# Which weight tiles of the last MLP are converted during attention, and which inside the MLP

## The chip, the cores and the metric

The kernel runs on one core of one Trainium2 chip. The metric is the device time of one execution in microseconds. A core has five engines that run their own instruction queues: TensorE (PE, matmul, with its weight loads shown apart as PEld), VectorE (DVE), ScalarE (ACT), GpSimd (POOL) and SyncE (SP, which here only issues DMAs). Each queue is worked off in the order in which it was written.

## The reference

Attention with a local window and 32 global tokens, a gated MLP with a convolution along the sequence, and a Fourier mixing stage with a second MLP. What this case touches is the last stage:

```python
def _moe2_ref(x, w_ch1, w_ch2):              # x: 4 x 576 x 512
    X = np.fft.fft(np.fft.fft(x, axis=1), axis=2)
    u = x + np.real(X)
    mu = np.mean(u, axis=-1, keepdims=True)
    var = np.mean((u - mu) ** 2, axis=-1, keepdims=True)
    un = (u - mu) / np.sqrt(var + 1e-06)
    ch = np.maximum(un @ w_ch1, 0.0) @ w_ch2  # 512 x 2048, 2048 x 512
    return u + ch
```

All weights arrive as 64-bit floats, and the kernel itself turns them into float32.

## The kernel before, in words

**Weight tiles.** The weights of the last MLP are 32 tiles, numbered 0 to 31: 0 to 15 are blocks of `w_ch1`, 16 to 31 of `w_ch2`. A tile arrives as 128 x 512 64-bit numbers (512 KB) and becomes two float32r halves, a rounded part and the remainder (512 KB as well), so that three matmuls give a product of nearly float32 accuracy. I call that a conversion. It is `unpack` (through `from_f64`) and `put`: on ACT L164, L167 and L200, on POOL L165, on DVE L171, L172 and L201. So it takes three instructions each of ACT and DVE, one of POOL.

**Where tiles are converted.** Twelve tiles are converted during attention, one in every second step (`keep_load`, `keep_make`, `keep_store`), and parked in DRAM as `kept`. Later `fetch_c` brings a kept tile back by a DMA that POOL issues (L724, `w_v<-kept`), finished, while a tile that was not kept comes in raw by a DMA that SP issues (L179), and `make_c` converts it.

**The boundary.** After attention, the end of the first MLP (`m_g1`, `m_conv`, `m_gate`, `m_g2`), the Fourier transforms of the four batches (`fft`, b = 0 to 3) and the first steps of the last MLP (`c_g1(v)`, then `c_g2(v - 2)`) are interleaved. A transform uses two banks of PSUM, `ps_s` and `ps_t`, in turn: a group of matmuls fills one, ACT and DVE (L665 and L666, L672 and L673) or DVE alone (L686, L689, L696, L699) empty it. The steps v = 0 to 4 (`NCONV`) of the last MLP carry the transforms of batches 1 to 3 and the conversions of tiles 8 to 19:

```python
order = [x for v in range(4) for x in (16 + v, 8 + v)] + [12, 13, 14, 15]
...
            for x in order[len(order) * v // NCONV:len(order) * (v + 1) // NCONV]:
                make_c(x)
```

From then on the last MLP is matmuls alone: 128 steps, eight chunks of 272 tokens by 16 hidden blocks. `c_g1(v)` multiplies by tile m = v mod 16 into the bank `ps_pv` or `ps_g`, ACT (L791) and DVE (L792) turn that into `hdt`, and `c_g2(v)` multiplies `hdt` by tile 16 + m. `ln` prepares the next chunk beside it (L745 to L773).

**Buffers.** Tiles 20 to 31 live in `fp`, in the slots of the transform's own constants and work tiles: 20 to 24 in those of `c2`, `s2`, `fh`, `fl` and `ff`, 25 and 26 in that of `c1`, 27 and 28 in that of `s1`, 29 to 31 in that of `ab`. They can be loaded only when the last transform has done with them. Tiles 16 to 19 live in `lw`, which takes over the space of the first MLP's work tiles. While the last MLP runs, the conversion's temporary is one of three places in `misc`.

**What sets the order.** SP and PE run in the order of the code up to the end of attention. Behind that a scheduler orders every engine's queue, by priorities (conversions of the last MLP, `cv`, 200; `fft` 100; `cev` 400) and its own idea of durations, so a change of the code can move instructions far from it.

Of the kernel before, what the change touches and what calls it, by code (L numbers as in the profile page):

```python
# [11 lines left out]
F32R = mybir.dt.float32r  # L12
BF16 = mybir.dt.bfloat16
I32 = mybir.dt.int32
# [16 lines left out]
SOLO = 8  # L31
LAG_G2 = 3
NCONV = 5
KEEP0, KEEP1 = 10, 20
NPB, NHB = 3, 3
MT = [(0, 92), (92, 92), (184, 90)]

# [88 lines left out]
def fused_kernel(ctx: ExitStack, tc: tile.TileContext, d, out):  # L126
    nc = tc.nc
    pe, act, dve, gp, sp = nc.tensor, nc.scalar, nc.vector, nc.gpsimd, nc.sync

    def pri(c):  # L130
        k = PRIORITY.get(c, 0)
        return tc.high_priority(offset=k) if k else nullcontext()

    def prio(c):
        def deco(f):
            def g(*a, **k):
                with pri(c):
                    return f(*a, **k)
            return g
        return deco  # L140
# [15 lines left out]
    def f32(ap):  # L156
        return ap.bitcast(F32)

    def bits(ap):
        return ap.bitcast(I32)  # L160
# [28 lines left out]
    def unpack(pool, t, *how):  # L189
        if mags:  # L190
            mag = mags.pop(0)
            mags.append(mag)
        else:
            mag = pool.tile([128, 512], F32, tag="mag", name="mag", bufs=2)
        from_f64(t.rearrange("p (c b) -> p c b", b=2), mag, *how)
        return mag
# [7 lines left out]
    def rows_of(w, m):  # L204
        return bits(w)[128 * m:128 * m + 128, :]
# [4 lines left out]
    def c_src(i):  # L210
        return cols_of(d["ch1"], i) if i < 16 else rows_of(d["ch2"], i - 16)
# [15 lines left out]
    mp = left.enter_context(tc.tile_pool(name="mp", bufs=2))  # L227
# [14 lines left out]

    def keep_tile(i, lag):
        k, odd = divmod(i - KEEP0 - lag, 2)
        return None if odd or not 0 <= k < 32 - KEEP1 else KEEP1 + k

    @prio("keep")
    def keep_load(x):
# [194 lines left out]
    w_raw, w_in, w_out = {}, {}, {}  # L443
# [181 lines left out]
    fp = right.enter_context(tc.tile_pool(name="fp", bufs=1, side="right"))  # L625
# [85 lines left out]
    ch1, ch2 = {}, {}  # L711

    def c_slot(i):
        return (wp, f"w{i}") if i < 16 else (lw if i < 20 else fp, f"v{i}")

    @prio("cv")
    def fetch_c(i, n=1):
        pool, tag = c_slot(i)
        if i not in kept:
            w_raw[i] = fetch(pool, tag, c_src(i))  # L720
            return
        t = pool.tile([128, n, 2, 512], F32R, tag=tag, name="w_" + tag)
        for j in range(n):
            gp.dma_start(t[:, j], kept[i + j])  # L724
            ch2[i + j - 16] = t[:, j]

    @prio("cv")
    def make_c(i):
        if i not in kept:
            t = put(*c_slot(i), unpack(mp, w_raw.pop(i), gp, True))  # L730
            (ch2 if i > 15 else ch1)[i % 16] = t

    ln_t, dead = {}, {}

    def ln(c):
# [96 lines left out]
    for u in range(ulast + 1, NM + LAG_G2):  # L832
# [15 lines left out]
        k = u - (NM - 8)  # L848
# [21 lines left out]
    for v in range(128 + 2):  # L870
        c, m = divmod(v, 16)
        if v < NCONV:
            while done * NCONV < nstep * (v + 1):
                step(f3)
                done += 1
                if nstep - done == 6:
                    for i in range(20, 25):
                        fetch_c(i)
            for x in order[len(order) * v // NCONV:len(order) * (v + 1) // NCONV]:
                make_c(x)  # L880
            if v == NCONV - 1:
                for i, n in ((25, 2), (27, 2), (29, 3)):
                    fetch_c(i, n)
                dead[1] = frp.tile([128, 4, 546], F32, tag="u", name="u")
        if m == (NCONV if c == 0 else 4) and c + 1 < 8:
            lnq.append(ln(c + 1))
        step(lnq)
        c_g1(v)
        c_g2(v - 2)
# [43 lines left out]
```

## Time and profile before

| | |
|---|---|
| time, median of 3 runs | 844.3 us (840.43 to 846.37) |
| time of the profiled execution | 842.18 us |
| its span, first to last instruction | 840.4 us |
| PE busy | 788.0 us (94%) |
| DVE busy | 460.1 us (55%) |
| ACT busy | 373.8 us (44%) |
| POOL busy | 197.9 us (24%) |
| mean granted clock of TensorE | 0.968 |

The shares are averages over stages that are limited by different things. Attention with the first MLP takes about 340 us, the boundary reaches from there to 471 us, and the rest is the last MLP. PE's clock is given as a share of 2.4 GHz; 0.50 is the lower of its two levels, 1.2 GHz.

### The profile page before, as it was taken

The numbers are of one execution on the slowest core, as the hardware profiler recorded it, in microseconds if no ns is written. First come the engines' busy times: TensorE is split into PE (matmuls) and PEld (weight loads), VectorE is DVE, ScalarE is ACT, GpSimd is POOL, SyncE is SP. The second block draws the span as 40 slices with busy tenths as digits, with TensorE's granted clock in tenths as the row PEclk, the third lists the DMA queues.
The fourth block names the chain that finished last, engine by engine and source line by source line (L and its number), as shares of the span: only waits on it lengthen the run. The fifth ranks groups of instructions, "written<-read, shape, count | busy, mean of one in ns | idle before, by whom it ended". The sixth has DMA issues, their size and how long they took to land.

```text
span 840.4 us, 16106 instructions
## 1 busy us (share of the span) xinstructions
PE 788.0 (94%) x6436; PEld 739.7 (88%) x6436; DVE 460.1 (55%) x1202; ACT 373.8 (44%) x949; POOL 197.9 (24%) x274
## 2 busy tenths in 40 slices
PE   5667999999999999999888999999999999999997
PEld 3445888888898889998777999999999999999997
DVE  5877986777777776688989531222222122222212
ACT  5666777676676675467764132121211212121110
POOL 3535332222222221001123252040402204030100
PEclk9787999999999999999969999999999999999999
DMA  9452034132322303025422700000000000000000
GB/s 315 162 190 78 34 127 143 50 142 83 110 99 93 101 26 103 8 87 164 142 110 55 247 27 1 2 27 1 28 1 28 1 2 27 1 28 1 27 2 28
DMA packets 28843, 60.93 MB, mean 72 GB/s; under 512 B 2344, under 2 KB 19112, under 8 KB 28768
## 3 DMA queue, kind: packets, MB, share of 16 engines
q1 hardware_dynamic: 26208, 50.95, 17.8%
q0 software_dynamic: 2560, 8.94, 3.5%
q8 instruction: 51, 0.84, 0.4%
q14 instruction: 24, 0.20, 0.1%
HBM read 49.52 MB, written 10.75 MB: 72 GB/s over the span
## 4 chain that ended last, share of the span: by engine, by line
PE 55%; DVE 19%; DMA 12%; ACT 10%; issue 2%; SPq 1%; POOL 0%; DVEq 0%; ACTq 0%
PE ps_a L143 25%; PE ps_g L143 14%; PE ps_pv L143 12%; DMA raw_r<-in_ch_dram 6%; PE ps_s L143 3%; DMA raw_w<-in_w_in_dram 3%; ACT pb L314 2%; DVE mag L171 2%; PE ps_t L143 2%; DVE y L487 2%; DVE pb L302 2%; DVE mag L172 2%; DVE w_w L201 1%; DVE y L488 1%; DVE g L507 1%
## 5 line engine op out<-in xcount | busy, mean ns | idle before, releaser
L143 PE MATMUL ps_a<-hdt,w_v 128*128 128x272 f32 x1536 | 214.6, 288 | 0.3 <-DVE w_v L201 0.3
L143 PEld LDWEIGHTS ps_a<-hdt,w_v 128*128 128x128 f32 x1536 | 201.5, 189 | 0.6 <-DVE w_v L201 0.6
L143 PE MATMUL ps_g<-xh,w_w 128*128 128x274 f32 x512 | 115.2, 304 | 3.3 <-ACT h L476 3.3
L325 POOL TENSOR_SCALAR pb<-pb,sm 128x224 f32<-128x224 f32 x128 | 76.5, 614 | 155.6 <-DVE sm L320 125.0
L143 PE MATMUL ps_a<-g,w_w 128*128 128x272 f32 x768 | 111.6, 292 | 0.1
L143 PE MATMUL ps_pv<-chl,w_w 128*128 128x272 f32 x768 | 108.0, 289 | 0.0
L143 PE MATMUL ps_g<-chl,w_w 128*128 128x272 f32 x768 | 107.8, 288 | 0.0
L143 PEld LDWEIGHTS ps_a<-g,w_w 128*128 128x128 f32 x768 | 101.5, 190 | 1.1 <-issue 0.5
L143 PEld LDWEIGHTS ps_pv<-chl,w_w 128*128 128x128 f32 x768 | 101.4, 190 | 0.0
L143 PEld LDWEIGHTS ps_g<-chl,w_w 128*128 128x128 f32 x768 | 100.7, 188 | 0.0
L143 PEld LDWEIGHTS ps_g<-xh,w_w 128*128 128x128 f32 x512 | 86.8, 193 | 11.7 <-issue 6.2
L792 DVE SCALAR_TENSOR_TENSOR hdt<-ps_pv,hdt 128x272 fp32r<-128x272 f32 x64 | 28.1, 440 | 123.2 <-ACT hdt L791 123.2
L792 DVE SCALAR_TENSOR_TENSOR hdt<-ps_g,hdt 128x272 fp32r<-128x272 f32 x64 | 28.0, 438 | 113.0 <-ACT hdt L791 113.0
L791 ACT ACTIVATE hdt<-ps_g 128x272 fp32r<-128x272 f32 x64 | 25.4, 397 | 137.3 <-PE ps_g L143 132.7
L791 ACT ACTIVATE hdt<-ps_pv 128x272 fp32r<-128x272 f32 x64 | 25.3, 396 | 137.4 <-PE ps_pv L143 133.1
L143 PE MATMUL ps_g<-xl,w_w 128*128 128x274 f32 x256 | 75.2, 294 | 0.0
L813 POOL TENSOR_TENSOR misc<-misc,u 128x272 f32<-128x272 f32 x28 | 19.3, 721 | 213.0 <-DVE misc L812 213.0
L314 ACT ACTIVATE pb<-pb,sm 128x224 f32<-128x224 f32 x128 | 60.3, 473 | 19.9 <-DVE sm L302 19.7
L143 PE MATMUL ps_s<-qk 64*128 64x224 f32 (+1 forms) x144 | 39.1, 427 | 13.2 <-DVE smg L396 6.1
L165 POOL TENSOR_SCALAR mag<-mag 128x512 f32<-128x512 f32 x36 | 24.5, 682 | 110.5 <-ACT mag L164 109.7
L143 PEld LDWEIGHTS ps_g<-xl,w_w 128*128 128x128 f32 x256 | 49.3, 193 | 0.0
L487 DVE SCALAR_TENSOR_TENSOR y<-h,convw,y 128x272 f32<-128x272 f32 x64 | 33.8, 529 | 25.0 <-ACT y L486 24.7
(207 smaller groups left out, 1269.9 us busy)
## 6 DMA issues: line engine op xcount, KB each, us to landing
qk<-in_qk_dram SPq DMA_DIRECT2D x16, 592.0 KB, 5.8
raw_w<-in_ch_dram SPq DMA_DIRECT2D x16, 512.0 KB, 3.7
raw_r<-in_ch_dram SPq DMA_DIRECT2D x12, 512.0 KB, 4.8
kept<-w_o SPq DMA_DIRECT2D x12, 512.0 KB, 3.0
w_v<-kept POOLq DMA_DIRECT2D x12, 512.0 KB, 4.8
v<-in_v_dram SPq DMA_DIRECT2D x8, 640.0 KB, 4.4
out_dram<-misc SPq DMA_DIRECT2D x32, 136.0 KB, 1.7
raw_w<-in_w_in_dram SPq DMA_DIRECT2D x8, 512.0 KB, 6.5
```

The source lines that it names most:

```text
L143: return pe.matmul(o, a, b, start=start, stop=stop)
L165: (clamp or dve).tensor_scalar(mag, mag, TOP, 2.0, op0=ALU.min, op1=ALU.max)
L171: dve.scalar_tensor_tensor(val, val, 3, tail, op0=ALU.logical_shift_left, op1=ALU.bitwise_or)
L172: dve.scalar_tensor_tensor(val, head, -(2**31), val, op0=ALU.bitwise_and, op1=ALU.bitwise_or)
L201: dve.tensor_sub(t[:, 1], val, f32(t[:, 0]))
L302: anchor[i] = dve.tensor_tensor_reduce(out=pbs(i)[h][:, a, 0:224], in0=sb[h][:, a], in1=mask[:, 2 * (i % 2) + a], scale=-0.125, scalar=3.0 ...
L314: act.activation(p, p, AF.Exp, bias=sm[:, k:k + 1], scale=-1.0, accum_out=sm[:, 4 + k:5 + k])
L325: gp.tensor_scalar(p, p, sm[:, k:k + 1], 1.0, op0=ALU.mult, op1=ALU.mult)
L487: dve.scalar_tensor_tensor(y, hb[:, cc - 1:cc - 1 + HS], convw2[:, m, 0:1], y, op0=ALU.mult, op1=ALU.add)
L791: act.activation(hd[:, 0], o, AF.Relu)
L792: dve.scalar_tensor_tensor(hd[:, 1], o, 0.0, f32(hd[:, 0]), op0=ALU.max, op1=ALU.subtract)
L813: (dve if c == 7 else gp).tensor_add(o, o, u_t[b][:, e, HS * half:HS * half + HS])
```

## The change

Twelve tiles are still converted during attention and parked, at the same steps, but they are 16 to 24 and 29 to 31, where they were 20 to 31. Tiles 16 to 19 now come back as kept tiles, so `make_c` has nothing to do for them. Tiles 25 to 28 come in raw in pairs, through SP (`fetch_cs`), and are converted in the slot in which they landed (`make_cs`): all values of a pair are first unpacked into places of `misc`, then the two finished tiles are written over the raw ones. The two conversions are written into the MLP steps v = 5 and v = 7.

```diff
-KEEP0, KEEP1 = 10, 20
+KEEP0 = 10
+KEPT = list(range(16, 25)) + [29, 30, 31]
...
     def keep_tile(i, lag):
         k, odd = divmod(i - KEEP0 - lag, 2)
-        return None if odd or not 0 <= k < 32 - KEEP1 else KEEP1 + k
+        return None if odd or not 0 <= k < len(KEPT) else KEPT[k]
...
+    @prio("cv")
+    def fetch_cs(i, k):
+        raw = fp.tile([128, k, 1024], I32, tag=f"v{i}", name="raws")
+        for j in range(k):
+            sp.dma_start(raw[:, j], rows_of(d["ch2"], i + j - 16))
+        w_raw[i] = raw
+
+    @prio("cv")
+    def make_cs(i, k):
+        raw = w_raw.pop(i)
+        vals = [unpack(mp, raw[:, j], gp, True) for j in range(k)]
+        t = fp.tile([128, k, 2, 512], F32R, tag=f"v{i}", name="ws")
+        for j in range(k):
+            act.copy(t[:, j, 0], vals[j])
+            dve.tensor_sub(t[:, j, 1], vals[j], f32(t[:, j, 0]))
+            ch2[i + j - 16] = t[:, j]
...
             if v == NCONV - 1:
-                for i, n in ((25, 2), (27, 2), (29, 3)):
-                    fetch_c(i, n)
+                for i in (25, 27):
+                    fetch_cs(i, 2)
+                fetch_c(29, 3)
                 dead[1] = frp.tile([128, 4, 546], F32, tag="u", name="u")
+        if v in (5, 7):
+            make_cs(20 + v, 2)
```

The scheduler's answer moves more than these lines. In the names below, `raw_w12` is raw tile 12, `w_w12` the finished one, and numbers behind the last underscore only tell buffers apart; in the changed kernel every line is 1 higher up to line 731, and 18 higher behind the two new functions.

The first place is DVE's queue at the end of the transform of batch 1, from the last piece of `ab` that the transform needs to the first emptying of its result. Before:

```order
L673 TENSOR_TENSOR ab_4961<-ps_s_5013,ab_4961 90x256
L648 TENSOR_TENSOR fl_5119<-ff_5117,fh_5118 128x548
L507 TENSOR_TENSOR g_4856<-y_4826,g_4856 128x272
L649 TENSOR_TENSOR ff_5117<-u_3692 128x548
L201 TENSOR_TENSOR w_w7_4930<-mag_4924,w_w7_4930 128x512
L696 SCALAR_TENSOR_TENSOR u_2602<-u_2602,ps_s_5065 128x273
```

The same place in the changed kernel:

```order
L674 TENSOR_TENSOR ab_4961<-ps_s_5013,ab_4961 90x256
L649 TENSOR_TENSOR fl_5111<-ff_5109,fh_5110 128x548
L173 SCALAR_TENSOR_TENSOR misc_4937<-raw_w12_4844,misc_4937 128x512
L508 TENSOR_TENSOR g_4856<-y_4826,g_4856 128x272
L202 TENSOR_TENSOR w_w7_4930<-mag_4924,w_w7_4930 128x512
L172 SCALAR_TENSOR_TENSOR misc_4937<-misc_4937,raw_w13_4872 128x512
L650 TENSOR_TENSOR ff_5109<-u_3692 128x548
L202 TENSOR_TENSOR w_w12_5404<-misc_4937,w_w12_5404 128x512
L172 SCALAR_TENSOR_TENSOR misc_4937<-misc_4937,raw_w11_4796 128x512
L173 SCALAR_TENSOR_TENSOR misc_4937<-raw_w13_4872,misc_4937 128x512
L697 SCALAR_TENSOR_TENSOR u_2602<-u_2602,ps_s_5083 128x273
```

Conversions of tiles 11, 12 and 13, which stood far behind this transform, now stand ahead of its last emptyings.

The second place is SP's queue behind the last raw tile of `w_ch1`. Before:

```order
L179 DMA raw_w15_4922<-in_ch1_dram 128x4x256
L179 DMA raw_v17_4940<-in_ch2_dram 128x1024
L179 DMA raw_v19_4944<-in_ch2_dram 128x1024
L179 DMA raw_v16_4938<-in_ch2_dram 128x1024
L179 DMA raw_v18_4942<-in_ch2_dram 128x1024
```

In the changed kernel, where `raws_5523` are tiles 27 and 28 and `raws_5520` tiles 25 and 26:

```order
L180 DMA raw_w14_4895<-in_ch1_dram 128x4x256
L180 DMA raw_w15_4922<-in_ch1_dram 128x4x256
L738 DMA raws_5523<-in_ch2_dram 128x1024 x2
L738 DMA raws_5520<-in_ch2_dram 128x1024 x2
L832 DMA out_0_dram<-misc_4937 128x272 x32
```

The four raw loads of tiles 16 to 19 are gone, and the pair that is used second is loaded first.

The third place is DVE's queue in the last MLP, around the preparation of the second chunk (L754 before, L772 now, which needs a PE result, `ps_t`). Before:

```order
L748 TENSOR_TENSOR hdt_4372<-u_5562,hdt_4372 128x272
L792 SCALAR_TENSOR_TENSOR hdt_4372<-ps_g1_5768,hdt_4372 128x272
L754 TENSOR_TENSOR u_5562<-u0_4074,ps_t_5649 128x1088
L792 SCALAR_TENSOR_TENSOR hdt_4372<-ps_pv_5800,hdt_4372 128x272
L792 SCALAR_TENSOR_TENSOR hdt_4372<-ps_g1_5827,hdt_4372 128x272
```

In the changed kernel, where `ws_5568` are the finished tiles 25 and 26:

```order
L766 TENSOR_TENSOR hdt_4372<-u_5530,hdt_4372 128x272
L810 SCALAR_TENSOR_TENSOR hdt_4372<-ps_g1_5766,hdt_4372 128x272
L172 SCALAR_TENSOR_TENSOR misc_4937<-misc_4937,raws_5520 128x512
L173 SCALAR_TENSOR_TENSOR misc_4937<-raws_5520,misc_4937 128x512
L772 TENSOR_TENSOR u_5530<-u0_4074,ps_t_5647 128x1088
L172 SCALAR_TENSOR_TENSOR misc_4937<-misc_4937,raws_5520 128x512
L173 SCALAR_TENSOR_TENSOR misc_4937<-raws_5520,misc_4937 128x512
L748 TENSOR_TENSOR ws_5568<-misc_4937,ws_5568 128x512 x2
```

The second tile of the pair is unpacked only behind L772, and both finished tiles behind that.

## Rows read from the trace of the kernel before

**Rows 1.** The page: busy times, and the span in 40 slices.

```profile
PE 788.0 (94%) x6436; PEld 739.7 (88%) x6436; DVE 460.1 (55%) x1202; ACT 373.8 (44%) x949; POOL 197.9 (24%) x274
...
PE   5667999999999999999888999999999999999997
...
DVE  5877986777777776688989531222222122222212
...
PEclk9787999999999999999969999999999999999999
```

**Rows 2.** Stretches: us; PE, PEld, DVE, ACT, POOL busy (count); PE clock; DMA, GB/s.

```profile
398.00:421.20 23.20, 19.35 (x148) 17.88 (x146) 23.11 (x47) 17.44 (x34) 2.28 (x3) 1.00 0.47 147
412.00:421.40 9.40, 5.83 (x41) 4.97 (x40) 9.31 (x21) 4.36 (x10) 0.00 (x0) 1.00 0.48 145
421.40:435.30 13.90, 12.94 (x51) 10.54 (x52) 10.90 (x21) 9.95 (x20) 3.93 (x5) 0.51 0.32 130
421.40:470.65 49.25, 45.96 (x303) 41.20 (x303) 44.16 (x86) 23.62 (x47) 15.08 (x19) 0.86 0.30 102
...
470.65:482.00 11.35, 11.35 (x93) 11.35 (x92) 3.08 (x7) 1.50 (x4) 3.73 (x7) 1.00 0.81 275
```

**Rows 3.** Timeline of PE: start us, duration us, instructions [idle before, releaser].

```profile
417.78 1.38 PE L143 MATMUL ps_s<-s,ab 92*128 92x274 f32 x9 [0.28 <-DVE u L699]
421.43 0.33 PE L143 MATMUL ps_s<-c,fl 128*92 128x258 f32 x1 [2.27 <-DVE u L699]
...
458.39 0.27 PE L143 MATMUL ps_t<-co,fh 1*90 1x258 f32 x1
...
463.19 1.67 PE L143 MATMUL ps_a<-hdt,w_v 128*128 128x272 f32 x12
...
469.50 1.32 PE L143 MATMUL ps_t<-c,ab 92*1 92x274 f32 x9
...
480.91 0.42 PE L143 MATMUL ps_t<-hdt,ones 128*128 128x272 f32 x2
```

**Rows 4.** Timeline of DVE.

```profile
420.86 0.42 DVE L699 SCALAR_TENSOR_TENSOR u<-u,ps_s 128x271 f32<-128x271 f32 x1
...
481.37 1.29 DVE L754 TENSOR_TENSOR u<-u,ps_t 128x1088 f32<-128x1088 f32 x1 [1.64 <-PE ps_t L143]
```

**Rows 5.** Chain that ended last, 360 to 480: start us, us, what.

```profile
411.10 0.60 DVE w_w L201
...
418.97 6.67 DMA raw_v<-in_ch_dram
```

**Rows 6.** DMA issues, 380 to 490: issuer, KB each, median us to landing.

```profile
w_v<-kept POOLq DMA_DIRECT2D x12, 512.0 KB, 4.8
raw_w<-in_ch_dram SPq DMA_DIRECT2D x11, 512.0 KB, 3.7
raw_v<-in_ch_dram SPq DMA_DIRECT2D x4, 512.0 KB, 6.3
```

**Rows 7.** ACT and DVE: a cast of the chunk, and groups of conversions, 398 to 462.

```profile
482.69 1.10 ACT L755 CAST chl<-u 128x1088 fp32r<-128x1088 f32 x1 [0.17 <-DVE u L754]
...
L200 ACT CAST w_w<-misc 128x512 fp32r<-128x512 f32 x8 | 5.0, 621 | 5.6 <-DVE misc L172 5.6
...
L201 DVE TENSOR_TENSOR w_w<-misc,w_w 128x512 fp32r<-128x512 f32 x8 | 5.4, 676 | 0.4 <-ACT w_w L200 0.4
```

**Rows 8.** Stretches around other falls of PE's clock, columns as in Rows 2.

```profile
378.00:379.70 1.70, 0.00 (x0) 0.00 (x0) 1.70 (x5) 1.65 (x3) 0.00 (x0) 1.00 0.72 240
380.60:384.00 3.40, 3.40 (x18) 3.40 (x17) 2.47 (x6) 3.08 (x8) 1.00 (x1) 0.52 0.34 86
31.90:39.20 7.30, 7.28 (x35) 5.46 (x36) 6.00 (x21) 5.66 (x15) 2.31 (x3) 0.50 0.39 130
```

**Rows 9.** Timeline of POOL.

```profile
458.57 0.57 POOL L724 DMA_DIRECT2D w_v<-kept  x1 [0.54 <-PE ps_t L143]
```

## The prediction

> **What bounds the kernel now.** I read the slices first [rows 1]: from the 23rd on (462 us) PE is at 9 in every slice but the last, and DVE falls to 1 or 2. That stage is PE's own, and nothing on DVE, ACT or POOL can shorten it. Since attention converts twelve tiles before and after, and at the same steps, what can change lies in the 20th to 22nd slice (399 to 462 us), where DVE stands at 9, 8 and 9, PE falls to 8, and in the 21st PE's clock to 6. The stretches show why [rows 2]: from 398 to 421.2 DVE is busy 23.11 of 23.20 us, so whatever stands in its queue there is late by the sum of all that stands ahead. PE pays at the end of it: from 412 to 421.4 it works 5.83 of 9.40 us. The last wait, 2.27 us, ends at 421.43 [rows 3] with DVE's L699, which runs at 420.86 [rows 4]: the transform of batch 2 cannot write into `ps_s` until DVE has emptied it of the last product of batch 1. I call this point B. Behind the wait PE's clock is 0.51 for 13.9 us, until 435.3 [rows 2]. From B to the end of the last transform (469.50 plus its 1.2 us of issue, about 470.65 [rows 3]) PE is busy 45.96 of 49.25 us.
>
> So the boundary loses in three ways: the wait at B, 3.3 us of small waits behind it (49.25 - 45.96), and the slow clock: work that took PE 12.94 us at half speed, of which half, 6.4 us, is the loss.
>
> **The change, part by part.** In attention nothing changes: same number, same steps, same size of load and store. That is 0.
>
> *DVE's queue ahead of B.* The conversions of tiles 16 to 19 are gone, 4 x 3 = 12 instructions of DVE. But the ones that stay have moved. I count the instructions of L171, L172 and L201 (one higher now) in DVE's queue. Before, 10 stand between the reciprocal of `ln(0)` (L773) and the L699 that releases B, and 33 behind it. Now 24 stand ahead and 7 behind. So 14 more stand ahead of B, 26 fewer behind. One instruction takes 0.60 us of the queue [rows 5] (0.68 from start to end [rows 7], with some overlap). DVE has no idle time there to take them in, 0.09 us of 23.2 [rows 2]. So B moves by 14 x 0.60 = 8.4 us, to about 429.8; with the longer duration it would be 9.5.
>
> What does PE do meanwhile? Its queue now has one item more ahead of B, the twelve matmuls of `c_g2(0)`, whose tile 16 comes back finished. Its space is free at about 419, when the first raw loads into it were on their way before [rows 5]; four loads then took 6.3 us in the median [rows 6], so it lies there by 427. Twelve matmuls at 11.35 / 93 = 0.122 us [rows 2] are 1.5 us, taken off the work behind B. Together: +8.4 - 1.5 = **+6.9 us**, from +6.9 to +8.0.
>
> *Behind B.* DVE now has 26 x 0.60 = 15.6 us less to do, so it no longer holds PE. The small waits of 3.3 us could go. But two things are late next. First, the transforms of batches 2 and 3 now stand in PE's queue with little between them (before, steps of the last MLP separated them), and with two banks each group of matmuls waits for the one before last to be emptied. An emptying is two instructions of 0.42 us [rows 4] and some signalling, nine matmuls are 1.1 us; over the 22 groups I estimate 0.1 us each, 2 us. Second, `c_g2(4)` now stands only 24 matmuls behind the last use of `c2`, where there were 36, and its tile 20 can be loaded only then. Before, `c2` was free at 458.4, POOL issued at 458.57 and PE used the tile at 463.19 without a wait [rows 3, 9]: 4.8 us, which is also the median of such loads [rows 6]. Now it is about 24 x 0.122 plus a microsecond of emptying, 4 us, so 1 us of wait. Sum 3.0 us against 3.3: **-0.3 us**, from -3.3 to +1.5.
>
> The Trainium skill, page "DMA: Bandwidth & Descriptors", section "Anatomy of one DMA", gives a DMA issued by POOL about 2 us plus its bytes at 436 GB/s; for 512 KB I estimate 3.2 us from it, which would leave this wait of 1 us out and make the sum smaller by that. The trace disagrees: 4.8 us [rows 6].
>
> *The clock.* It falls again, since PE now idles longer ahead of B than before. How long it stays low behind B is the largest unknown. The nearest rows: after an idle stretch of 1.70 us it was at 0.52 for 3.40 us, and elsewhere, with PE fully busy, at 0.50 for 7.30 us [rows 8]; here it was 13.9 us [rows 2]. I take 5 us, between these two rows, which costs 2.5, against 6.4 before: **-3.9 us**, from -6.4 (back at once) to 0 (as long as before).
>
> *Tiles 25 to 28 in the MLP.* Their twelve DVE instructions (7.2 us), twelve of ACT and four of POOL lie where DVE is busy 3.08 of 11.35 us [rows 2]; as load they cost nothing. But they are a chain with a due time. From the end of the last transform, PE has 92 matmuls until it needs tile 25: 92 x 0.122 = 11.2 us. DVE's queue puts L772 ahead of the second tile's unpacking, and both finished tiles behind that. L772 waits for the two `ones` matmuls, number 79 and 80 in that count, so for 9.8 us (before, 480.91 - 470.65 + 0.4 = 10.7 [rows 3]). It takes 1.2 us [rows 4]; then two unpacking steps 1.2, the cast on ACT (which has the 1.10 us of L773 ahead of it [rows 7], done in that time) 0.6, a second one beside the remainder, 0.6: ready at 9.8 + 1.2 + 1.2 + 0.6 + 0.6 = 13.4 us. PE waits 2.2 us. The loads: SP issues 27 and 28 first; 25 and 26 follow when `c1` is free, at the end of the last transform, beside 29 to 31 of POOL. Four raw loads took 6.3 us in the median [rows 6], so they have landed by about 7, in time for the unpacking at 11. If they land at 10, ACT, which stands waiting for them in its queue, holds `hdt` of two steps, and PE waits 3 us more. Tile 27 comes out just ahead of its use. **+2.2 us**, from 0 to +5.
>
> SP's queue is free of other work there: behind the raw loads stand only the stores of the first chunk. POOL has two unpacking instructions ahead of `ln`'s sums, 1.3 us, with some 10 us to spare.
>
> **The sum** is 6.9 - 0.3 - 3.9 + 2.2 = **+4.9 us** on the profiled execution's 842.2 us (span 840.4 and 1.8 around it), so 847.1. That execution lies 2.1 us below the median of the three runs; on the median it is 844.3 + 4.9 = **849.2 us**, +0.6%. One per cent, 8.4 us, is about what a measurement of this kernel can tell from no change: its three runs spread over 5.9 us.
>
> **The rivals.**
>
> *The clock stays low.* Behind B the low stretch lasts as long as before, and the wait of 2.2 us at tile 25 brings another of 3.4 us, as the idle 1.70 us did [rows 8]. Then the clock's term is 0 and 1.7 us come on top: 4.9 + 3.9 + 1.7 = +10.5, 854.8 us, measurably slower. For it: PE idles longer ahead of B than it did. Against it: the other two stretches were 3.4 and 7.3 us. It passes 1% when the low stretch behind B lasts 12 us without the second one, 8.6 us with it. 22%.
>
> *A wash or a little better.* The clock is back at once, no small waits, tile 25 ready in time: 6.9 - 3.3 - 6.4 + 0 = -2.8, 841.5 us. Each of the three would have to go to its end. With one or two of them the time is 843 to 847. 17%.
>
> *The load counts, not its place.* DVE sheds 12 instructions in the stretch that it bounds, so the boundary is shorter by 12 x 0.60 = 7.2 us: 837.1. For it: DVE at 8 and 9 in those slices. Against it: the queue is worked off in its order, and B stands behind more work. It would be true if the wait at B were not DVE's. It reaches 1% only where the clock's 6.4 us go as well. 7%.
>
> The Trainium skill, page "Perfetto Trace Analysis", section "Identifying the Most-Contended Engine", says to find the engine with the highest occupancy in a regime and to relieve it first; by that rule the time would be that of this rival, 837.1 us. The trace bears it out in so far as DVE is the fullest here, 23.11 of 23.20 us [rows 2], and speaks against it where the wait at B ends with one instruction of DVE, and not with the end of its work.
>
> *The change doesn't do what it says.* If kept tiles 16 to 19 came too late for `c_g2(0)` to `c_g2(3)`, PE would wait for POOL's loads where it waited for conversions: the four need the space of the first MLP's work tiles, free about 420, and land by 431. B is at 429.8, so at most 2 us, in the range already.
>
> **How the numbers follow.** The forecast, 849.2 us, has 52%; the clock's rival 22%; the wash 17%; the load 7%; 2% for what I don't see. The range, 842 to 857, reaches from the wash to a little above the clock's rival and takes in the spread of the runs. Faster by over 1%: 6%, from the load's rival with the clock's gain. Slower by over 1%: 22% and the upper edge of the forecast, 25%. Within 1%: 69%.
>
> **What would show it.** In the changed kernel's trace: PE's first product of the transform of batch 2 starts 8 us later than at 421.4, with a wait for DVE's L700 ahead of it; behind it DVE has idle time, and the end of the last transform comes within 0 to 5 us of 470.65. PE's clock row shows a low stretch shorter than 13.9 us behind that point. At the first matmul on `ws`, about 11 us later, PE waits 2 us for DVE's L748. The forecast is wrong if PE passes B near 421, if PE's clock stays low beyond 12 us behind B, or if PE waits at tile 25 for raw data.

## The result, and the profile after

The changed kernel takes 855.2 us (median of four executions, 853.5 to 861.6) against 845.3 us: a ratio of 1.0145, 95% interval 1.0114 to 1.0175. That is 10 us, twice the 4.9 us forecast, and slower by more than one per cent. The range, 842 to 857, holds it, but the case with the best chance, no change beyond one per cent, did not come.

The page of the changed kernel, its busy times and slices, answers to [rows 1]:

```profile
PE 789.6 (93%) x6436; PEld 740.6 (87%) x6436; DVE 464.4 (55%) x1202; ACT 373.3 (44%) x949; POOL 204.3 (24%) x274
...
PE   5767999999999899999699899999999999999997
...
DVE  5877987776868676789966652222222122222212
...
PEclk9787999999999999999889989999999999999999
```

PE is down to 6 in the 20th slice (404 to 426 us), where it stood at 8, and to 8 in the 23rd (468 to 490), where it stood at 9; PE's clock is at 8 in the slice behind that. So the loss sits in two places. To price them I cut both traces at three marks: the first product of the normalisation (`ones`, behind which the boundary begins), the start of the last transform's last group, which I call T (469.50 before [rows 3]; the prediction counts from its end, 1.15 us later), and the end.

PE's timeline in the changed kernel, the marks and the two places:

```profile
371.53 0.41 PE L144 MATMUL ps_t<-hdt,ones 128*128 128x272 f32 x2
...
421.67 2.02 PE L144 MATMUL ps_a<-g,w_w 128*128 128x272 f32 x8
...
428.92 3.06 PE L144 MATMUL ps_a<-hdt,w_v 128*128 128x272 f32 x12 [1.73 <-ACT raw_w L168]
...
431.78 0.42 PE L144 MATMUL ps_s<-c,fl 128*92 128x258 f32 x1
...
472.69 1.30 PE L144 MATMUL ps_t<-c,ab 92*1 92x274 f32 x9
...
483.58 0.41 PE L144 MATMUL ps_t<-hdt,ones 128*128 128x272 f32 x2
...
489.98 5.71 PE L144 MATMUL ps_a<-hdt,ws 128*128 128x272 f32 x24 [4.49 <-DVE ws L748]
```

| | before | after | difference | forecast |
|---|---|---|---|---|
| start to first `ones` | 371.43 | 371.53 | +0.1 | 0 |
| first `ones` to T | 98.07 | 101.16 | +3.1 | +2.7 (6.9 - 0.3 - 3.9) |
| T to the end of the span | 370.90 | 379.01 | +8.1 | +2.2 |
| span | 840.4 | 851.7 | +11.3 | +4.9 |

The boundary came out near the forecast in the sum, though not in its parts. Behind T, where the in-place tiles are converted, the cost is almost four times its term. Stretches of the changed kernel (columns as in [rows 2]): the one ahead of point B, the one from B to T, the wait at tile 25 with the 11.65 us ahead of it, and the seven microseconds from just ahead of its end:

```profile
371.53:431.78 60.25, 48.15 (x333) 44.83 (x332) 56.91 (x106) 46.04 (x95) 18.76 (x19) 0.91 0.53 162
431.78:472.69 40.91, 39.23 (x280) 35.05 (x280) 26.77 (x57) 8.70 (x22) 5.58 (x6) 0.97 0.26 76
...
473.84:485.49 11.65, 11.65 (x94) 11.43 (x92) 6.02 (x11) 5.64 (x11) 4.68 (x8) 1.00 0.73 262
485.49:489.98 4.49, 0.00 (x1) 0.00 (x0) 3.72 (x5) 2.25 (x4) 2.48 (x1) 0.85 0.00 0
488.80:495.80 7.00, 5.82 (x27) 5.82 (x28) 5.73 (x7) 3.29 (x6) 3.84 (x4) 0.53 0.01 2
```

The same two stretches up to T in the kernel before:

```profile
371.43:421.43 50.00, 44.20 (x322) 41.34 (x320) 45.62 (x89) 38.75 (x82) 6.67 (x9) 0.97 0.53 164
421.43:469.50 48.07, 44.80 (x294) 40.37 (x295) 43.90 (x86) 23.62 (x47) 13.96 (x18) 0.86 0.28 96
```

B comes 10.25 us later, counted from `ones`, and 7.2 us of that come back behind it, where DVE no longer stands at 43.9 of 48 us and the clock is at 0.97 instead of 0.86. The low clock is not gone, though: before, it lay behind B [rows 2]; now most of it lies ahead of B:

```profile
416.90:423.80 6.90, 5.14 (x21) 4.82 (x21) 6.39 (x12) 3.19 (x8) 4.82 (x2) 0.51 0.00 0
...
427.20:434.00 6.80, 5.08 (x21) 4.53 (x21) 6.80 (x14) 2.84 (x6) 4.01 (x2) 0.50 0.82 293
```

Behind T, PE does nothing for 4.49 us and then works at 0.50, the lower of the clock's two levels (1.2 GHz): 0.53 in the mean of the stretch from 488.80 to 495.80, with 27 matmuls in 7 us.

What the other engines do at these places, DVE, POOL and ACT of the changed kernel:

```profile
430.09 0.42 DVE L700 SCALAR_TENSOR_TENSOR u<-u,ps_s 128x271 f32<-128x271 f32 x1
...
483.80 0.69 DVE L173 SCALAR_TENSOR_TENSOR misc<-raws,misc 128x512 int32<-128x512 int32 x1
484.41 1.28 DVE L772 TENSOR_TENSOR u<-u,ps_t 128x1088 f32<-128x1088 f32 x1
485.60 0.68 DVE L172 SCALAR_TENSOR_TENSOR misc<-misc,raws 128x512 int32<-128x512 int32 x1
486.32 0.69 DVE L173 SCALAR_TENSOR_TENSOR misc<-raws,misc 128x512 int32<-128x512 int32 x1
487.75 2.78 DVE L748 TENSOR_TENSOR ws<-misc,ws 128x512 fp32r<-128x512 f32 x2 [0.74 <-ACT ws L747]
...
494.57 1.29 DVE L748 TENSOR_TENSOR ws<-misc,ws 128x512 fp32r<-128x512 f32 x2 [0.39 <-ACT ws L747]
```

```profile
417.15 4.82 POOL L166 TENSOR_SCALAR misc<-misc 128x512 f32<-128x512 f32 x2 [3.60 <-ACT misc L165]
424.23 2.19 POOL L725 DMA_DIRECT2D w_v<-kept  x4 [2.26 <-issue]
...
486.90 2.48 POOL L774 TENSOR_TENSOR chl<-u,chl 128x1088 fp32r<-128x1088 f32 x1 [6.46 <-ACT chl L773]
```

```profile
479.08 0.67 ACT L165 ACTIVATE misc<-raws 128x512 f32<-128x512 f32 x1
```

The queue is as the prediction read it: L772, then the second tile's unpacking, then the two finished tiles (L748). What it did not see is in the row at 487.75: these two L748 take 2.78 us, the next two 1.29. POOL's L774 runs from 486.90 to 489.38, and the first L748 ends just behind that, as PE's start at 489.98 shows.

### The profile page after: what moved, and what is told of

Same layout as the page of the kernel before. It is cut to its first block, busy times and chain, and to the rows that moved or that the text cites. A ratio compares the mean times of both kernels' runs of the same rounds, so it can differ in the third digit from the quotient of the medians.

```text
span 851.7 us, 16110 instructions
## 1 busy us (share of the span) xinstructions
PE 789.6 (93%) x6436; PEld 740.6 (87%) x6436; DVE 464.4 (55%) x1202; ACT 373.3 (44%) x949; POOL 204.3 (24%) x274
## 4 chain that ended last, share of the span: by engine, by line
PE 52%; DVE 18%; DMA 12%; ACT 10%; issue 6%; POOL 1%; SPq 0%; DVEq 0%; ACTq 0%; POOLq 0%
PE ps_a L144 24%; PE ps_g L144 13%; PE ps_pv L144 11%; DMA raw_r<-in_ch_dram 7%; DVE mag L172 2%; ACT pb L315 2%; PE ps_s L144 2%; DVE y L488 2%; DVE pb L303 2%; DVE mag L173 2%; DVE y L489 2%; DMA raw_w<-in_ch_dram 1%; PE ps_t L144 1%; DMA raw_w<-in_w_out_dram 1%; DVE w_w L202 1%
## 5 line engine op out<-in xcount | busy, mean ns | idle before, releaser
L144 PE MATMUL ps_a<-hdt,w_v 128*128 128x272 f32 x1152 | 162.2, 289 | 1.9 <-ACT raw_w L168 1.7
L144 PEld LDWEIGHTS ps_a<-hdt,w_v 128*128 128x128 f32 x1152 | 151.8, 190 | 2.7 <-issue 2.2
L144 PE MATMUL ps_a<-hdt,ws 128*128 128x272 f32 x384 | 55.3, 296 | 4.5 <-DVE ws L748 4.5
L144 PEld LDWEIGHTS ps_a<-hdt,ws 128*128 128x128 f32 x384 | 52.2, 197 | 4.7 <-DVE ws L748 4.7
L166 POOL TENSOR_SCALAR mag<-mag 128x512 f32<-128x512 f32 x36 | 25.5, 710 | 106.4 <-ACT mag L165 105.5
```

The lines of the kernel that those rows point to most:

```text
L144: return pe.matmul(o, a, b, start=start, stop=stop)
L166: (clamp or dve).tensor_scalar(mag, mag, TOP, 2.0, op0=ALU.min, op1=ALU.max)
```

## The experiments

The theory: the boundary costs 3 us, as forecast, and the in-place tiles 8, because tile 25's chain ends 4.5 us too late, and PE's clock falls for it. The main rival: the low clock, or the work of the conversions behind T, would cost the same without that wait.

The table gives each kernel's median, its ratio to the kernel before (with its interval), and of the profiled execution the marks. "Uptake" is the moment, counted from T, at which ACT takes the second tile's raw data (its third L165 behind T); "waits" are PE's, for the tile or for `hdt` held up with it; the low clock is that of these waits, read from stretches of 1 us; it can begin inside the wait. The kernel before, run beside each of them, had medians of 842.7 to 845.3 us, so two kernels are best compared by their ratios.

| run | median us | ratio (95%) | `ones` | to T | T to end | uptake | waits | low clock |
|---|---|---|---|---|---|---|---|---|
| after | 855.2 | 1.0145 (1.0114-1.0175) | 371.5 | 101.2 | 379.0 | 6.4 | 4.5 | 7 |
| e1 | 846.8 | 1.0035 (1.0020-1.0049) | 373.6 | 100.0 | 371.8 | - | 0 | 0 |
| e2 | 852.0 | 1.0083 (1.0056-1.0110) | 375.2 | 103.7 | 372.6 | 7.5 | 0 | 0 |
| e3 | 845.8 | 1.0036 (1.0011-1.0060) | 366.0 | 97.6 | 379.3 | 8.6 | 1.3 + 4.1 | 3.4 |
| e4 | 851.3 | 1.0092 (1.0075-1.0109) | 372.5 | 99.5 | 377.3 | 6.3 | filled, 0.5 later | 0 |
| e5 | 838.5 | 0.9945 (0.9921-0.9969) | 366.8 | 98.5 | 372.3 | 6.4 | 0 | 0 |
| e6 | 853.8 | 1.0122 (1.0078-1.0166) | 375.0 | 102.5 | 379.5 | 9.2 | 1.7 + 2.3 + 1.4 | 3.4 |
| e7 | 854.7 | 1.0141 (1.0100-1.0182) | 369.1 | 104.2 | 377.2 | 6.3 | 4.5 | 3.2 |
| e8 | 855.9 | 1.0155 (1.0108-1.0201) | 368.8 | 100.6 | 383.2 | 11.2 | 3.7 + 3.1 | 7 + 3.5 |
| e9 | 851.3 | 1.0103 (1.0058-1.0148) | 371.6 | 101.2 | 376.8 | 8.8 | 0.7 + 1.6 + 1.6 | 0 |
| e10 | 848.1 | 1.0072 (1.0043-1.0100) | 372.8 | 99.8 | 373.3 | 6.5 | 0, 1.0 later | 0 |
| e11 | 851.8 | 1.0084 (1.0055-1.0114) | 374.9 | 100.8 | 374.5 | 9.4 | 0.2 + 0.4 + 0.8 | 0 |
| e12 | 857.0 | 1.0162 (1.0126-1.0197) | 368.0 | 102.3 | 382.5 | 10.6 | 3.0 + 3.0 | 7 + 3.4 |

Executions with the same twelve tiles in attention reach the first `ones` anywhere from 368.0 to 375.2 us, so a single profile's span says little; the two later columns and the medians are what is compared.

**e1, no in-place conversion.**

```diff
-    raw = fp.tile([128, k, 1024], I32, tag=f"v{i}", name="raws")
+    t = fp.tile([128, k, 2, 512], F32R, tag=f"v{i}", name="ws")
     for j in range(k):
-        sp.dma_start(raw[:, j], rows_of(d["ch2"], i + j - 16))
+        gp.dma_start(t[:, j], kept[i + j - 4])
...
-        if v in (5, 7):
-            make_cs(20 + v, 2)
```

> Leaves out the conversion of tiles 25 to 28: their places are filled with finished copies of tiles 21 to 24, loaded by POOL, so the output is not the reference's. Everything up to the end of the last transform is as in the changed kernel. Theory (the chain of tile 25 ends too late for PE: 4.5 us of wait, and the low clock behind it, some 3 us, is a consequence of that wait): the wait at the first product of step 9 and the low stretch behind it are both gone, and the time falls by 7 to 7.5 us, from 855.2 to about 848. Rival A (the low clock comes by itself, because PE has worked for long): the wait goes, the 3 us of low clock stay, 851. Rival B (whatever feeds step 9 is late, since the loads stand behind one another): a wait for a DMA takes its place, 853 to 856.

846.8 us, T to the end 371.8, no wait and no low clock. PE's timeline of e1 at the first two products that stood still in the changed kernel:

```profile
483.00 1.66 PE L144 MATMUL ps_a<-hdt,ws 128*128 128x272 f32 x12
...
486.27 1.67 PE L144 MATMUL ps_a<-hdt,ws 128*128 128x272 f32 x12
```

The theory holds: by the ratios the in-place conversion costs 1.1%, 9 us, of the 1.45%; all the rest of the change costs 0.35%, 3 us.

**e2, other four tiles in place**, needed later.

```diff
-KEPT = list(range(16, 25)) + [29, 30, 31]
+KEPT = list(range(16, 28))
...
-                for i in (25, 27):
+                for i in (28, 30):
                     fetch_cs(i, 2)
-                fetch_c(29, 3)
+                fetch_c(25, 3)
...
-        if v in (5, 7):
-            make_cs(20 + v, 2)
+        if v in (7, 9):
+            make_cs(21 + v, 2)
```

> Same count of tiles converted in attention and in place, but tiles 16 to 27 come finished and tiles 28 to 31 are converted in place, behind the MLP steps 7 and 9, so the first of them is needed three steps later: 3 x 24 x 0.122 = 8.8 us. Theory (due time): the 4.5 us of wait are covered by 8.8, the low clock behind it does not come, 855.2 - 7.5 = about 848, and PE reaches the first product of the transform of batch 2 at 431.8 as before this edit. Rival A (a new wait): tiles 25 to 27 now come through POOL into the space that is free only at the end of the last transform (473.8); at 6.4 us for a load they land after 480 to 486, PE wants tile 25 at 485.5, so up to 2 us of wait and perhaps the low clock behind it, 849 to 852. Rival B (the chain is late by its length, not by its due time: DVE is held by the normalisation's instructions of the second chunk again): the wait stays over 3 us, 853 to 855.

The wait and the low clock are gone in the profile and T to the end is 372.6, as the theory has it. The median is not: 852.0 instead of 848. Two things were wrong. "Three steps later" is less than 8.8 us: in the changed kernel PE's queue has two further groups of the first weight ahead of tile 25, so that 92 matmuls stand between the last transform and it, and 140 here, 48 x 0.125 = 6 us. And with uptake at 7.5 the tile was ready just as PE wanted it (both 19 us behind T), so an execution with later data waits again; e11 shows one. The profiled execution itself (853.2 us) did not wait: its excess lies ahead of T, and what put it there the runs don't show.

**e3, the in-place half alone.** Eight tiles come finished, 16 to 19 are converted at the boundary as before.

```diff
-KEPT = list(range(16, 25)) + [29, 30, 31]
+KEPT = list(range(20, 25)) + [29, 30, 31]
```

> One half of the change alone: tiles 20 to 24 and 29 to 31 come finished out of attention (eight instead of twelve), 16 to 19 are converted at the boundary as in the kernel before, 25 to 28 in place. DVE's queue up to the first product of the transform of batch 2 is that of the kernel before, so that point should lie where it lay relative to the end of the last MLP (before: 421.4; earlier by what attention saves with four conversions fewer, which no row prices; I say 0 to 3 us). Theory (the wait of tile 25 is counted from the end of the last transform and has nothing to do with the lateness ahead of it): PE waits 4 to 5 us at tile 25, the clock falls behind it, +7.5 us on the kernel before, 845.3 + 7.5 - (0 to 3) = 850 to 853. Rival (the wait is a consequence of the boundary's lateness, through loads and ACT's queue): with the boundary as before the wait is under 2 us, 844 to 847.

The wait is there with the boundary of the kernel before (97.6 us to T): 4.1 us at tile 25, behind 1.3 on `hdt`, and T to the end is 379.3. PE's timeline of e3:

```profile
481.87 4.80 PE L144 MATMUL ps_a<-hdt,ws 128*128 128x272 f32 x24 [4.12 <-DVE ws L748]
```

So it does not come of the lateness ahead of it, and the rival falls. The time, 845.8, lies below what I expected, for a reason that I had priced too low: attention ends at 366.0 with eight tiles instead of 371.5 with twelve. Over all runs it is 366.4 (two) against 372.0 (mean of twelve, 368.0 to 375.2): 5.6 us for four tiles.

**e4, extra products in the wait.**

```diff
         c_g1(v)
+        if v == 11:
+            o = bank("s")[:, 0:HS]
+            for k in range(36):
+                mm(o, ch1[0][:, 0, 0:128], hid[11][:, 0], k == 0, k == 35)
         c_g2(v - 2)
```

> 36 extra products whose result nobody reads stand in PE's queue ahead of tile 25, 36 x 0.122 = 4.4 us, about as long as PE waits there; the chain of tile 25 is untouched. It tells whether idling is what lets the clock fall. Theory (it is the idle 4.5 us): PE is busy up to tile 25, the clock stays at its upper level behind it, and the time falls by the 2.5 to 3 us of the low stretch, 852.5. Rival A (the clock falls by itself there): no change, 855, and the low stretch is seen at 488 to 495 all the same. Rival B (the extra products run at the low clock themselves or push everything behind them): slower by up to 4 us, 859.

851.3 us, 4 us less (4.5 by the ratios), with 36 matmuls more. The products on tiles 25 and 26 in PE's timeline of e4, and the same seven microseconds as above:

```profile
489.37 3.29 PE L144 MATMUL ps_a<-hdt,ws 128*128 128x272 f32 x24
```

```profile
488.80:495.80 7.00, 6.49 (x50) 6.05 (x49) 4.87 (x8) 3.95 (x7) 3.08 (x3) 1.00 0.00 0
```

24 products take 3.29 us instead of 5.71, and 50 matmuls fit where 27 did. So the low clock was a consequence of the idle wait. In these rows it cost 2.4 us, beside 4.49 us of wait; the medians differ by more, within their intervals.

**e5, eight tiles finished, the later four in place**: e2's edit with `KEPT = list(range(20, 28))`.

> Tiles 20 to 27 come finished out of attention, 16 to 19 are converted at the boundary as in the kernel before, 28 to 31 in place behind the MLP steps 7 and 9: the in-place half of the change with the due time of the earlier run on the other four tiles. Theory (due time): eight instead of twelve tiles in attention leave 5.4 us sooner (366.0 against 371.5 at the first product of the normalisation), the in-place half now costs nothing, so 845.3 - 5.4 = 838 to 840, faster than both kernels by 0.5 to 0.8%. Rival A (the load counts: DVE, ACT and the loads behind the end of the last transform cost PE something wherever they stand): part of the wait of 4.1 us and of the low clock stays, 842 to 846. Rival B (the new wait: tiles 25 to 27 come by POOL into a space free at the end of the last transform): 1 to 3 us at tile 25, 840 to 843.

838.5 us, ratio 0.9945 (0.9921 to 0.9969): faster than both kernels, as expected. T to the end is 372.3, the boundary that of the kernel before, and attention is 5 us shorter. Neither rival shows.

**e6, L772 behind the finished tiles.**

```diff
-        dve.tensor_sub(cf, ut, mu[:, None, :].to_broadcast([128, 4, HS]))
+        cen = dve.tensor_sub(cf, ut, mu[:, None, :].to_broadcast([128, 4, HS]))
+        if c == 1:
+            tc.add_manual_dep(cen.ins, ws_done[25].ins.name, ...)
```

(`ws_done[25]` is the last L748 of tiles 25 and 26.)

> Same tiles, loads and due times as the changed kernel; the centring of the second chunk (L772, with ACT's cast and POOL's L774 behind it) is made to follow the finished tiles 25 and 26 on DVE. Theory (the chain is too long by what stands in it): without L772 (1.28 us ahead of the second tile) and without POOL's L774, beside which two L748 took 2.78 us where two others took 1.29, the tile is finished some 3 us sooner, PE waits 1 to 1.5 us instead of 4.5, and the low clock behind it is shorter or gone: 855.2 - 3 to - 7, 848 to 852. Rival (the raw loads are what is late: the second tile's landed at 479.1): the two L748 end at the same time as before but for 1 us, the time stays within 854 to 856.

853.8 us: beside the rival's 854 to 856, and above the theory's 848 to 852. The profiled execution, 858.8 us, is the slowest of four; its rows show what held it. PE, DVE and ACT of e6:

```profile
488.70 1.77 PE L144 MATMUL ps_pv<-chl,w_w 128*128 128x272 f32 x12 [1.66 <-DVE hdt L815]
...
494.81 4.79 PE L144 MATMUL ps_a<-hdt,ws 128*128 128x272 f32 x24 [2.31 <-DVE ws L748]
```

```profile
494.06 1.29 DVE L748 TENSOR_TENSOR ws<-misc,ws 128x512 fp32r<-128x512 f32 x2 [0.74 <-ACT ws L747]
```

```profile
486.67 0.66 ACT L165 ACTIVATE misc<-raws 128x512 f32<-128x512 f32 x1 [2.67 <-DMA raws<-in_ch_dram]
```

The theory is right about L774: without it beside them the two L748 take 1.29 us. But here the raw data came 2.8 us later than in the changed kernel (uptake 9.2 instead of 6.4), ACT stood 2.67 us waiting for it, and the `hdt` of the step behind it in ACT's queue was late as well, 1.66 us of PE.

**e7, the boundary with 15 conversion instructions moved behind B.**

```diff
+                if done == 13:
+                    for i in range(11, 16):
+                        fetch_c(i, after=anch[1])
...
-        if 0 <= k - 3 < 8:
+        if 0 <= k - 3 < 3:
             fetch_c(8 + k - 3)
```

(`anch[1]` is the last instruction of batch 1's transform.)

> The other half: the raw loads of tiles 11 to 15 are paced behind the last instruction of the transform of batch 1, so that 15 conversion instructions of DVE, 9 us, stand behind the point at which PE starts the transform of batch 2, instead of ahead. Tiles in attention and in place as in the changed kernel. Theory (the order in DVE's queue set that point): DVE releases it 9 us sooner, 50 us behind the first product of the normalisation instead of 60, and the end of the last transform comes 2 to 4 us sooner (98 to 100 behind it instead of 102): 851 to 853. Rival A (tile 16's load holds PE as well: it landed some 57 us behind that product, as its space came free late): the wait moves to the product on tile 16, and the end of the last transform stays at 101 to 102, 854 to 856. Rival B (DVE now holds PE behind that point, as in the kernel before): 854 to 857.

The transform of batch 2 starts 53.8 us behind `ones` instead of 60.25 (with a group on `ps_t`; its group on `ps_s`, which came first before, starts at 57.6), and nothing comes of it: 854.7 us, and T is reached at 104.2. PE's timeline and a stretch of e7:

```profile
422.97 0.36 PE L144 MATMUL ps_t<-s,fl 128*92 128x256 f32 x1 [1.04 <-DVE u L709]
...
450.77 0.35 PE L144 MATMUL ps_t<-co,fl 1*92 1x258 f32 x1 [1.03 <-DVE fl L653]
...
455.52 0.49 PE L144 MATMUL ps_s<-s,fl 128*92 128x256 f32 x1 [1.56 <-DVE u L709]
```

```profile
452.00:466.00 14.00, 12.28 (x53) 10.19 (x54) 5.70 (x13) 2.83 (x7) 2.12 (x4) 0.52 0.27 82
```

Between 448 and 456 PE now waits four times for DVE (0.57, 1.03, 0.92 and 1.56 us), and behind these waits the clock is at 0.52 for 14 us. Rival B holds: DVE's work has to be done on one side of B or the other.

**e8, no wait for tile 16** (the first chunk's product on it uses a tile of the first weight).

```diff
-        w = ch2[m]
+        w = ch2[m] if v else ch1[0]
```

> The product that used tile 16 in the first chunk uses a finished tile of the first weight instead, so it waits for no load; its output is not the reference's. DVE's queue up to the release is unchanged. Theory (that release sets PE's start on the transform of batch 2, and the product on tile 16, running at half clock at 428.9 to 432.0, added 1.7 us to it): the start comes right behind DVE's release, 58.5 to 59 us behind the first product of the normalisation instead of 60.25, and the time falls by 1 to 2 us, 853.5. Rival A (PE would have waited for DVE in any case and the load cost nothing): same start within 0.5 us, 855. Rival B (tile 16's lateness also let the clock fall): the low stretch at 427 to 434 is missing, and the time falls by 3 us or more.

PE's timeline of e8 at B:

```profile
427.08 0.49 PE L144 MATMUL ps_s<-c,fl 128*92 128x258 f32 x1 [2.73 <-DVE u L700]
```

B lies 58.3 us behind `ones` instead of 60.25 (59.2 to 60.9 in the nine executions with this order in DVE's queue), so tile 16's late load cost B 2 us, as the theory has it. The time does not fall, 855.9: the boundary is 0.6 us shorter, and behind T this execution got its raw data at 11.2. What the 2 us are worth in the time this run doesn't show.

**e9, POOL's loads of tiles 29 to 31 held back** until tile 26's raw data is in use, and **e10, the same with e6's edit**.

```diff
-                fetch_c(29, 3)
...
             make_cs(20 + v, 2)
+            if v == 5:
+                fetch_c(29, 3)    # each load depends on the last clamp of make_cs
```

> Same tiles as the changed kernel; POOL's three loads of tiles 29 to 31 are issued only when the raw data of tile 26 has been clamped, instead of beside the four raw loads. Counted from the start of the last transform's last group (T), ACT took up tile 26's raw data at 6.3 to 6.4 in three executions, at 8.6, 9.2 and 11.2 in three others. Theory (the loads share the engines of the DMA, and the raw data is late for that): it is taken up at 4.5 to 5.5 every time, and no wait of PE on hdt comes of it; the two L748 still stand behind L772 and beside L774, so the wait on the tile stays at 4 to 4.5 us and the time at 853 to 855. Rival A (the raw loads are slow by themselves): taken up at 6 to 11 as before. Rival B (tiles 29 to 31 now come too late): a new wait of PE on them, 855 to 858.

> The same, and L772 of the second chunk behind the two finished tiles as in the run e6. Theory (the chain has three parts that each cost: raw data beside other loads, L772 in DVE's queue, L774 on POOL beside the last instruction): with all three gone the tile is finished some 5 us behind the uptake of the raw data, at T + 10 to 11, PE needs it at T + 12.5 (485.5 in the changed kernel), there is no wait and no low clock behind it, and T to the end is 372 us, as in the kernel without in-place work (371.8) and the one with the later four (372.6): 855.2 - 7 = 847 to 849. Rival (the loads are still late): the wait is 2 to 4 us with the low clock behind it, 852 to 854.

In e9 the uptake is at 8.8 with nothing else loading, so my theory falls and its rival A holds: the four raw loads come at different times by themselves. The time, 851.3, lies below the theory's 853 to 855: PE waits three times, and the clock doesn't fall. The tile comes 17.5 us behind T, as in the changed kernel (17.3), though the raw data came 2.4 us later: L772 and L774 set its end. In e10 the uptake is at 6.5, and there the chain without L772 and L774 fits. ACT, DVE, PE and POOL of e10:

```profile
479.04 0.67 ACT L167 ACTIVATE misc<-raws 128x512 f32<-128x512 f32 x1
```

```profile
483.72 1.29 DVE L755 TENSOR_TENSOR ws<-misc,ws 128x512 fp32r<-128x512 f32 x2 [0.39 <-ACT ws L754]
...
488.23 2.48 DVE L175 SCALAR_TENSOR_TENSOR misc<-raws,misc 128x512 int32<-128x512 int32 x1
```

```profile
485.22 3.15 PE L144 MATMUL ps_a<-hdt,ws 128*128 128x272 f32 x24
...
491.11 1.76 PE L144 MATMUL ps_g<-chl,w_w 128*128 128x272 f32 x12 [0.98 <-DVE hdt L822]
```

```profile
487.63 2.53 POOL L786 TENSOR_TENSOR chl<-u,chl 128x1088 fp32r<-128x1088 f32 x1 [1.79 <-ACT chl L785]
```

From the uptake to the first finished tile it is 5.4 us here (479.04 to 484.4), against 10.9 in the changed kernel (479.08 to about 489.95). PE does not wait for the tile, T to the end is 373.3, and the median, 848.1 us, is what the theory asked for. PE's one wait, 0.98 us, is for an `hdt` that stands in DVE's queue behind the L175 of 2.48 us, so the moved L786 still costs something, at another place.

**e11 and e12, e2 and the changed kernel once more**, no edit.

> The kernel of e2 once more, beside the changed kernel on one chip, since its 852.0 us lie 4 us above what its rows explain. Theory (the excess was the spread of four executions; the rows behind the last transform showed no wait and 372.6 us to the end): 847 to 849, 6 to 8 us below the changed kernel beside it. Rival (the other four tiles cost something ahead of the last transform): 851 to 853 again, 3 to 4 us below the changed kernel.

> The changed kernel once more, for that comparison and for the spread of its own terms. Theory: 854 to 856; from the start of the last transform's last group to the end 377 to 380 us, with a wait of 4 to 5 us at tile 25 or, where the raw data lands late, of 5 to 7 us in two pieces; the low clock behind it lasts 3 to 7 us. Rival (the wait and the low clock of the first profile were an accident): under 852, and 372 to 374 us from that start to the end.

e11 gives 851.8 again, so the rival's number, with a wait that e2's profile did not have: uptake at 9.4, 1.4 us of PE in three pieces, T to the end 374.5. That is 2.7 us of its excess over e1 (371.8); the other 2 us of that profile lie ahead of T, and whether they belong to the kernel stays open. e12 gives 857.0. ACT and PE of e12:

```profile
480.86 0.66 ACT L165 ACTIVATE misc<-raws 128x512 f32<-128x512 f32 x1 [1.31 <-DMA raws<-in_ch_dram]
```

```profile
482.89 3.09 PE L144 MATMUL ps_pv<-chl,w_w 128*128 128x272 f32 x12 [3.03 <-DVE hdt L810]
...
492.05 4.80 PE L144 MATMUL ps_a<-hdt,ws 128*128 128x272 f32 x24 [3.02 <-DVE ws L748]
```

Same kernel, later data: two waits of 3 us, a low stretch behind each, T to the end 382.5. The wait of the first profile was no accident; it was the mild form.

## Why the prediction was wrong

**The step that failed is the term "Tiles 25 to 28 in the MLP", +2.2 us, from 0 to +5.** The mechanism was the one named, a chain with a due time; its size was not. In the changed kernel's two profiles it measured 8.1 and 11.6 us against T to the end of before, and 9 us by the ratios of e1 and the changed kernel. Put in place of 2.2, the profiled sum is 4.9 - 2.2 + 8.1 = 10.8, where 11.3 was measured. Its parts:

- *The wait, 4.49 us instead of 2.2.* The tile was due 11.65 us behind the end of the last transform (forecast 11.2) and ready at 16.1 (forecast 13.4). I had the `ones` matmuls done at 9.8 and L772 behind them at once. They began at 9.74 and were done at 10.15, and L772 began at 10.57, right behind the first tile's unpacking in DVE's queue (L173 at 483.80): 0.8 us. Another 0.3 us went into the two unpacking steps and the cast, and 1.5 us came from L774: 2.78 us for two L748 instead of 1.29. I had written that POOL has "some 10 us to spare" and had not asked what POOL's own work does to DVE. e6 and e10 show both parts gone.
- *The low clock behind it*: 24 products took 5.71 us instead of e4's 3.29, so 2.4 us in the profiles, and 3.9 us between the medians of e4 and the changed kernel. It stood only in a rival, at 1.7 us, with a chance of 22%. e4 shows that the idle wait brings it; e1 and e5 have no wait and no fall; in e10, with a wait of 1.0 us, and in e9, with 0.7, 1.6 and 1.6, there was no fall either. Since the sum forecast a wait of 2.2 us, and [rows 8] show a fall behind an idle 1.70 us, it belonged in the sum, as a chance if not as a certainty. The wait and the fall make 6.9 of the 8.1 us; e1, with neither, has T to the end at 371.8 where before has 370.9, one profile each.
- *The raw loads.* The prediction took 7 us behind the end of the last transform and called 10 us the bad case, "PE waits 3 us more". In that count, 1.15 us less than from T, the uptake was at 5.2 to 5.3 in five of twelve profiles, at 6.3 in one and at 7.4 to 10.0 in six. The changed kernel's first profile was one of the five, so its 4.49 us owe nothing to this; e8 and e12 (10.0 and 9.4, with 3.7 and 3.0 us on `hdt`) are the bad case. Late data was common, and was left out of the sum.

**Ahead of B: right in kind, 1.9 us short.** DVE released B at 430.09 instead of 420.86, +9.2 us (forecast 8.4, or 9.5 by the longer duration). PE came another 1.3 us later: I let the twelve products on tile 16 fit into the wait, with the tile's space free at about 419. But the last product of the first MLP, behind which the space is free, ended at 423.69 (421.67 plus 2.02), where before it had ended at 417.50:

```profile
415.84 1.66 PE L143 MATMUL ps_a<-g,w_w 128*128 128x272 f32 x12
```

POOL issued the load at 424.23. In all nine executions with this order in DVE's queue the issue follows the end of that product by 0.5 to 0.6 us. The load itself took 4.6 us, as forecast (4.8 [rows 6]; PE's row at 428.92 names an ACT instruction that ended within 0.1 us of the landing, and in e2, e6 and e11 the same row names the load), and the products ran at half clock, 3.06 us instead of 1.5. e8 shows what the tile's lateness costs B, 2 us.

**Behind B: better than forecast.** From B to T 40.91 us instead of 48.07: -7.2, where -1.5 - 0.3 - 3.9 = -5.7 was forecast. PE's small waits there fell from 3.3 to 1.7 us, where I had kept 3.0, and the low clock lasted 2.2 us there, not 5, since it now began ahead of B. Over the executions with this order it lasted, behind B, from 0.4 us (e1) to 6.2 us (e12), which is part of why T comes anywhere between 99.5 and 103.7 us behind `ones`. The nine of them average 101.2, the three with the order of before 98.1: +3.1, forecast +2.7. That the two misses, one ahead of B and one behind, nearly cancel is luck.

**The rivals.** "The clock stays low" gave 854.8 us, close to the result by luck. Its first half is wrong: behind B the clock came back sooner than I took. Its second half, a fall behind the wait at tile 25, came true, behind a wait of twice the length. "The load counts, not its place" is refuted by the result, and by e7 from the other side: moving the load past B changes nothing either, as DVE binds behind it too. The last rival came true in small: tile 16 was late for `c_g2(0)`, and cost B the 2 us that this rival allowed (e8); otherwise the change did what it says.

**Attention at 0** holds for the change (twelve tiles both times); but it hid that a tile converted there is not free: 5.6 us for four, e3 and e5.

## What to carry to other kernels

A chain with a due time is priced by every instruction queued ahead of each of its steps on every engine, by what other engines run beside it, and by the late half of its loads, not by their median; if the sum then says that the tensor engine waits, the clock's fall behind the wait goes into the sum. Work taken off one side of a release on a full engine is paid on the other side (e7), so move it to a stage where that engine is empty and the due time is far: e5 does this with the last four tiles, and gains 0.55% where the change lost 1.45%.

## What the runs showed of the hardware

In these rows a DVE instruction with two inputs in SBUF stands still while a POOL instruction that began earlier runs on two. Two L748 took 1.29 us alone (e6, and the second pair above) and 2.78 us where L774 ran for 1.63 us beside them (487.75 to 489.38); in e10 one L175, 0.68 to 0.69 us elsewhere, took 2.48 us where L786 ran for 1.93 us beside it (488.23 to 490.16). Each time the excess is the time beside it, less a tenth or two: the instruction waits for POOL's to end, then runs. The other way round it looks alike: two of POOL's L166 took 4.82 us at 417.15, where DVE was busy almost without a break, and 0.61 us each at 478.54 and 479.83, where DVE was idle. The Trainium skill, page "SBUF — State Buffer", section "SBUF: two separate sides", says that the two share a port pair as an exclusive lock, held for a whole instruction, so that the loser blocks; these rows agree.

Four raw loads of 512 KB, issued by the same instructions at the same place, gave their third tile to ACT between 6.3 and 11.2 us behind T in twelve executions, with or without other loads beside them. SP issued that tile's load 1.7 us behind T in all twelve, and ACT took the tile up within 0.3 us of its landing, so the spread is the load's own. What decides it the runs don't show.
